# First feed-forward layer in blocks of 512 tokens, two blocks through half of the weights at a time

## The chip, the cores and the metric

The kernel runs on one core of a Trainium2 chip. The core's engines work side by side and meet at semaphores: TensorE (PE in the profile; PEld is its weight load), VectorE (DVE), ScalarE (ACT), GpSimd (POOL), and SyncE (SP), which here issues nearly all DMA transfers; 16 DMA engines carry them out. TensorE's results go to PSUM, eight banks of 512 float32 per partition. The metric is the device time of one execution in microseconds (us), of the slowest core; here there is only one.

## The reference

Attention with a forget gate, then two feed-forward layers, each over 2304 tokens of 512 features with 2048 hidden ones:

```python
def _attn_ref(q, k, v, f):            # 4 sequences, 8 heads, 576 tokens, 64 features per head
    scores = np.matmul(q, k.transpose(0, 1, 3, 2)) / np.sqrt(D)
    cum = np.cumsum(np.log(np.clip(f, 0.0001, 1.0)), axis=-1)
    decay = cum[:, :, :, None] - cum[:, :, None, :]
    scores = np.where(causal, -1000000000.0, scores + decay)
    ...
    return np.matmul(attn, v)         # attn: softmax of scores

def _moe_ref(x, w_in, w_out):         # layer one
    h = x @ w_in
    return (h * np.clip(h + 3.0, 0.0, 6.0) / 6.0) @ w_out

def _moe2_ref(x, w_in, w_out):        # layer two; beta = 1
    h = x @ w_in
    g = np.where(h >= 1, h, np.where(h <= -1, 0.0, (h + 1) ** 2 / 4.0))
    return g @ w_out
```

The weights come as 64-bit floats; the result is float32.

## The kernel before, in words

**Attention.** A sequence's 576 queries are cut into a first half of 256 (half 0) and the rest of 320 (half 1). `ORDER` lists the eight (sequence, half) groups in the order in which they are done. A group has four head pairs. An early pair (half 0) is one job: scores of both heads (`sc`), softmax on VectorE and ScalarE (lines 589 and 595), normalisation (`prob`, 667), transposes (`pt`, 682), and the product with v (`av`, 724). A late pair (half 1) is three jobs, with more scores and transposes and an `av` of ten matmuls. From `av` the pair's part of the next layer's input is written twice, rounded (`xt`, ACT line 371) and as the rest (DVE line 379). Score, transpose and `av` results take turns in two PSUM banks (`ps`); from step 34 on two more (`ps_b`) join them.

**Feed-forward.** Both layers are matrix products in fp32r, each factor split into a rounded part and its rest, so that three matmuls stand for one. The hidden features are 16 chunks of 128 (`NCH`). A step is one chunk of one block of tokens: `moe_h` makes `hp` (4 x 3 matmuls, line 811) and from it the gated `u` and its two parts `g`; `moe_o`, two steps later (`LAG`), adds the chunk's share to the block's output accumulators `o` (12 matmuls, line 852 in layer one, 859 in layer two). Layer one works in nine blocks of 256 tokens, layer two in four of 512 and one of 256. In layer one `hp` and `o` have a matmul width equal to the block (256); in layer two `hp` has 512 and `o` has the 512 output features. Finished accumulators go by `osb` to DRAM (`x2d`) and come back as layer two's input.

**Blocks 0 and 1** run interleaved, block 1 nine chunks behind (`STAG`); each of the others goes through all 16 chunks.

**Weights.** A chunk's input and output weights together fill one slot of `wsb`; there are 12, and 4 more when attention's buffers are free (`g7`, seven blocks done). The first time, a chunk comes raw as two halves of 64-bit numbers (`wraw`, 512 KB each) and is narrowed by one ScalarE and four VectorE operations (lines 428 to 439, tile `wr`), then rounded and split into the slot (`w`, one operation of each engine). `w_keep` stores the split chunk (`wf<-w`, 1 MB) if it is needed again; later loads are `w<-wf`. Layer two's halves are narrowed during layer one and kept in DRAM by GpSimd (`wf<-wr`).

**Order.** The program is written step by step, with attention's pieces dealt out between the half steps by their costs; `plan` then orders each engine's instructions by a list schedule with modelled costs (`graph`, `schedule`). The code below is that of the functions which the change touches; line numbers are the profile's.

Of the kernel before, what the change touches and what calls it, by code (L numbers as in the profile page):

```python
# [28 lines left out]
ORDER = ((0, 0), (1, 0), (2, 0), (0, 1), (1, 1), (3, 0), (2, 1), (3, 1))  # L29
# [8 lines left out]
SLOTS = 12  # L38
MORE = 16 - SLOTS
LAG = 2  # L40
STAG = 9
XT = 11
PRE0, PRE1 = 38, 106
WRAW = 4
AHEAD = 8100


def plan_weights(visits, avail):

# [185 lines left out]
def schedule(g, bw=330.0, fixed=3000.0, small=150.0):  # L235
# [20 lines left out]
    def when(k):  # L256
        t, need = ready[k], {}
        for name in g["users"][k]:
# [63 lines left out]
def tile_kernel(  # L322
# [71 lines left out]

    again = {}  # L400
# [688 lines left out]
```

## Time and profile before

| | us |
|---|---|
| median of 3 runs (1077.58 to 1081.18) | 1078.97 |
| the profiled execution, its own time | 1082.1 |
| its span, first to last instruction | 1080.1 |
| PE busy | 1028.2 (95%) |
| DVE busy | 597.6 (55%) |
| ACT busy | 544.6 (50%) |

The page's rows of 40 slices show the stages. A digit is a slice's busy share in tenths, PEclk the granted clock of TensorE:

```profile
PE   6796899989999999899999999999999999999998
DVE  6898995576677787678753447422422422332222
PEclk7697899999999999999999999999999999999999
DMA  6966595396596696865826035200200200010010
```

Each slice is 27 us. VectorE is fullest in the first six; TensorE from the fifth on. From about 580 us only feed-forward work is left, and layer two begins near 670 us. In the tables of stretches a row gives the stretch, its length, the busy us of PE, PEld, DVE, ACT and POOL with the number of instructions in brackets, then the granted clock, the share of the DMA engines and GB/s; where a line is named, only its engine's busy time is given. A matmul's own duration in a group overlaps its neighbours; what one costs in a dense stretch is read from the chain, where twelve in a row have one start and one length.

### The profile page before, as it was taken

What the parts mean: (1) busy time and instruction counts of PE and PEld (TensorE: products, weight loads), DVE (VectorE), ACT (ScalarE), POOL (GpSimd) and SP (SyncE); (2) the same over time, 40 slices, a digit from 0 to 9 for tenths busy, and PEclk for the clock granted to TensorE, in tenths of its full rate; (3) what the DMA queues carried; (4) which work ended last, traced back from release to release, by engine and by line L of the source; (5) the groups of instructions that cost most, each with busy time, mean ns of one, the idle gap of its engine ahead of it and who ended that gap; (6) DMA issues with size and microseconds to landing.
All of it is one profiled execution on the core that took longest, in us unless ns stands there. A gap on an engine that the chain in (4) does not pass through costs nothing.

```text
span 1080.1 us, 18043 instructions
## 1 busy us (share of the span) xinstructions
PE 1028.2 (95%) x6538; PEld 902.1 (84%) x6538; DVE 597.6 (55%) x1508; ACT 544.6 (50%) x1330; POOL 90.1 (8%) x223
## 2 busy tenths in 40 slices
PE   6796899989999999899999999999999999999998
PEld 4486799989888998798899999888888888888887
DVE  6898995576677787678753447422422422332222
ACT  5786775556556665556653235433333333333343
POOL 1100111011112111111111000000100100000000
PEclk7697899999999999999999999999999999999999
DMA  6966595396596696865826035200200200010010
GB/s 198 322 191 187 179 302 164 87 306 188 152 301 179 194 320 200 268 205 152 271 86 254 2 104 189 59 1 5 74 1 1 69 10 0 20 40 1 1 39 20
DMA packets 69784, 144.19 MB, mean 133 GB/s; under 512 B 11584, under 2 KB 38720, under 8 KB 65600
## 3 DMA queue, kind: packets, MB, share of 16 engines
q1 hardware_dynamic: 67136, 134.66, 40.5%
q0 software_dynamic: 2560, 8.39, 2.0%
q8 instruction: 51, 0.84, 0.3%
q14 instruction: 37, 0.30, 0.1%
HBM read 116.74 MB, written 26.29 MB: 132 GB/s over the span
## 4 chain that ended last, share of the span: by engine, by line
PE 74%; DMA 10%; DVE 8%; issue 2%; ACT 2%; SPq 0%; DVEq 0%; ACTq 0%
PE hp L811 32%; PE o L852 14%; PE o L859 10%; PE ps L859 8%; DMA kraw<-in_k 4%; PE av L724 3%; PE pt L682 3%; DMA dec<-ncum 3%; PE sc L638 2%; DMA x2d<-osb 1%; DVE prob L589 1%; DVE wr L436 1%; PE sc L613 1%; DMA wraw<-in_w 1%; DVE wr L439 1%
## 5 line engine op out<-in xcount | busy, mean ns | idle before, releaser
L811 PE MATMUL hp<-xt,w 128*128 128x256 f32 x1728 | 253.6, 291 | 3.4 <-DVE u L818 2.6
L852 PE MATMUL o<-g,w 128*128 128x256 f32 x1728 | 247.9, 289 | 1.4 <-ACT g L371 1.4
L811 PEld LDWEIGHTS hp<-xt,w 128*128 128x128 f32 x1728 | 227.7, 193 | 9.1 <-DVE u L818 1.8
L852 PEld LDWEIGHTS o<-g,w 128*128 128x128 f32 x1728 | 225.7, 192 | 4.9 <-ACT g L371 1.6
L811 PE MATMUL hp<-x,w 128*128 128x512 f32 (+1 forms) x960 | 211.2, 369 | 0.7 <-DVE u L822 0.7
L811 PEld LDWEIGHTS hp<-x,w 128*128 128x128 f32 x960 | 169.2, 188 | 33.5 <-DVE u L822 0.9
L822 DVE SCALAR_TENSOR_TENSOR u<-hp,u 128x512 f32<-128x512 f32 (+1 forms) x80 | 50.9, 638 | 210.2 <-ACT u L821 210.2
L379 DVE TENSOR_TENSOR g<-u,g 128x256 fp32r<-128x256 f32 (+1 forms) x224 | 112.3, 502 | 72.7 <-ACT g L371 72.1
L371 ACT ACTIVATE g<-u 128x256 fp32r<-128x256 f32 (+1 forms) x224 | 106.6, 476 | 87.5 <-DVE u L822 50.6
L820 ACT ACTIVATE u<-hp 128x512 f32<-128x512 f32 (+1 forms) x80 | 44.3, 554 | 196.5 <-PE hp L811 196.5
L859 PE MATMUL o<-w,g 128*128 128x512 f32 x480 | 124.8, 396 | 0.0
L859 PEld LDWEIGHTS o<-w,g 128*128 128x128 f32 x480 | 89.1, 188 | 19.8
L817 ACT ACTIVATE u<-hp 128x256 f32<-128x256 f32 x144 | 54.8, 380 | 99.7 <-PE hp L811 99.2
L595 ACT ACTIVATE prob<-prob,mx 128x384 f32<-128x384 f32 (+4 forms) x144 | 83.5, 581 | 34.6 <-DVE mx L589 33.6
L859 PE MATMUL ps<-w,g 128*128 128x512 f32 x384 | 100.3, 396 | 0.0
L818 DVE SCALAR_TENSOR_TENSOR u<-u,hp 128x256 f32<-128x256 f32 x144 | 60.0, 417 | 67.9 <-ACT u L817 67.3
L682 PE MATMUL pt<-ident,prob 128*128 128x128 f32 (+1 forms) x400 | 69.2, 293 | 21.5 <-DVE prob L667 6.9
L859 PEld LDWEIGHTS ps<-w,g 128*128 128x128 f32 x384 | 72.3, 189 | 17.5 <-ACT osb L869 0.3
L371 ACT ACTIVATE pt<-pt 128x512 f32<-128x512 f32 (+3 forms) x160 | 63.9, 432 | 25.5 <-PE pt L682 24.9
L589 DVE CUSTOM_DVE_ANT_0 prob<-sc,dec 128x256 f32<-128x256 f32 (+1 forms) x112 | 59.0, 535 | 24.7 <-PE sc L638 8.9
L682 PEld LDWEIGHTS pt<-ident,prob 128*128 128x128 f32 (+1 forms) x400 | 49.1, 149 | 27.3 <-ACT u L817 10.7
L724 PE MATMUL av<-pt,vv 128*64 128x320 f32 (+3 forms) x448 | 56.4, 381 | 1.1 <-DVE mx L589 1.1
(72 smaller groups left out, 958.9 us busy)
## 6 DMA issues: line engine op xcount, KB each, us to landing
wraw<-in_w SPq DMA_DIRECT2D x64, 512.0 KB
w<-wf SPq DMA_DIRECT2D x24, 1024.0 KB
dec<-ncum SPq DMA_DIRECT2D x45, 256.0 KB
kraw<-in_k SPq DMA_DIRECT2D x64, 144.0 KB
wf<-w SPq DMA_DIRECT2D x8, 1024.0 KB
wf<-wr POOLq DMA_DIRECT2D x32, 256.0 KB, 6.4
w<-wf SPq DMA_DIRECT2D x16, 512.0 KB
vv<-in_v SPq DMA_DIRECT2D x16, 320.0 KB
```

The lines of the kernel that those rows point to most:

```text
L371: nc.scalar.activation(out=out, in_=in_, func=AF.Copy)
L379: e.tensor_tensor(out=out, in0=in_, in1=hi.bitcast(F32), op=ALU.subtract)
L589: nc.vector.tensor_tensor_reduce(out=py[:, a:e], in0=s, in1=dc, scale=-0.125, scalar=mx[:, 2 * z:2 * z + 1] if x else 3.0e38, op0=ALU.add, ...
L595: nc.scalar.activation(out=py, in_=py, func=AF.Exp, scale=-1.0, bias=mx[:, 2 * z + x:2 * z + x + 1], accum_out=sm[:, z:z + 1],)
L682: nc.tensor.transpose(t[:nk, o:o + P], p[:, c:c + nk], ident)
L724: nc.tensor.matmul(t[y * D:(y + 1) * D, o:nq], lhsT=vv[:nk, y, c], rhs=rhs, start=c == 0, stop=c == nkc - 1,)
L811: nc.tensor.matmul(hp, lhsT=ws[:, a, k], rhs=x[:, bb, 0:w], start=(k == 0 and a == 0 and bb == 0), stop=(k == KD - 1 and bb == 1),)
L817: nc.scalar.activation(out=u, in_=hp, func=AF.Relu, bias=3.0, scale=1.0)
L818: nc.vector.scalar_tensor_tensor(out=u, in0=u, scalar=6.0, in1=hp, op0=ALU.min, op1=ALU.mult)
L822: nc.vector.scalar_tensor_tensor(out=u, in0=hp, scalar=1.0, in1=u, op0=ALU.max, op1=ALU.min)
L852: nc.tensor.matmul(o, lhsT=ws[:, a, KD + k], rhs=gg[:, bb], start=(n == 0 and k % 2 == 0 and a == 0 and bb == 0), stop=(n == NCH - 1 and b ...
L859: nc.tensor.matmul(acc[j][k], lhsT=gg[:, bb, k * P:(k + 1) * P], rhs=ws[:, a, KD:2 * KD].rearrange("p k n -> p (k n)"), start=(n == 0 and ...
```

## The change

Layer one gets the blocks 512, 512, 512, 256, 512. The first two go through half of the weights at a time: block 0 through chunks 0 to 7, block 1 through 0 to 7 and 8 to 15, block 0 through 8 to 15. So block 0's output is made in two parts, stored in two DRAM tensors and added when layer two reads them. All four groups of half 0 are attended first. Input and output weights have slots of their own, nine each (half the size), seven more each after attention; `w_keep` follows a chunk's second use. Layer one's outputs leave through `xt` buffers, and its four accumulators (`ps_o`) serve attention until the first step; after that attention has the two banks of `ps`. In `graph`, loads of raw weights and stores to `wf` count as ready only after the matmul written before them.

Line 811 becomes 822, 852 becomes 865, 371 becomes 378, 379 becomes 386, 436 and 439 become 439 and 442.

```diff
-T = 256
-NB = NT // T
+T1 = (512, 512, 512, 256, 512)
 T2 = (512, 512, 512, 512, 256)
+NB = len(T1)
 NB2 = NB + len(T2)
+WIDTH = T1 + T2
+FROM = [sum(T1[:j]) for j in range(NB)] + [sum(T2[:j]) for j in range(len(T2))]
...
-ORDER = ((0, 0), (1, 0), (2, 0), (0, 1), (1, 1), (3, 0), (2, 1), (3, 1))
+ORDER = ((0, 0), (1, 0), (2, 0), (3, 0), (0, 1), (1, 1), (2, 1), (3, 1))
...
-SLOTS = 12
-MORE = 16 - SLOTS
+SLOTS = (9, 9)
+OPEN = ((0, 0, 8), (1, 0, 8), (1, 8, 16), (0, 8, 16))
+LOOK = 5
 LAG = 2
-STAG = 9
+GO = 0
 XT = 11
-PRE0, PRE1 = 38, 106
-WRAW = 4
-AHEAD = 8100
-
-
...
+PRE = (17, 62)
+WRAW = 3
+AHEAD = 60000
+LEAD = (1, 1, 1, 1, 1, 1)
...
+    last = None
+    for k in range(n):
+        if eng[k] == "PE":
+            last = k
+        elif last is not None and type(ops[k]).__name__ == "InstDMACopy":
+            if any(x[0].startswith(held) for x in info[k][1]) if held else False:
+                deps[k].add(last)
...
-    ps_o = pool("ps_o", 1, PSUM)
     ps_h = pool("ps_h", 2, PSUM)
     ps_a = pool("ps", 2, PSUM)
-    ps_x = pool("ps_x", 1, PSUM)
-    ps_b = []
+    ps_o = pool("ps_i", 4, PSUM)
     turn = [0]
...
     def bank(name):
-        if name == "hp":
-            return ps_h.tile([P, 512], F32, tag="ps", name=name)
         turn[0] += 1
-        p = ps_b[0] if ps_b and turn[0] % 2 else ps_a
+        p = ps_h if name == "hp" else ps_o if turn[0] > 0 and turn[0] % 3 else ps_a
         return p.tile([P, 512], F32, tag="ps", name=name)
...
-    x2d = dram.tile([DM, NT], F32, name="x2d")
-    wf = [dram.tile([P, 2, 8, P] if c < NCH else [P, 8, P], F32, name=f"wf{c}") for c in range(2 * NCH)]
+    x2d = [dram.tile([DM, NT if x == 0 else T1[0]], F32, name=f"x2d{x}") for x in range(2)]
+    wf = [
+        [dram.tile([P, 2, 4, P] if c < NCH else [P, 4, P], F32, name=f"wf{c}_{x}") for x in range(2)]
+        for c in range(2 * NCH)
+    ]
...
-    wsb = [wpool.tile([P, 2, 8, P], F32R, name=f"w{s}") for s in range(SLOTS)]
+    wsb = [[wpool.tile([P, 2, 4, P], F32R, name=f"w{x}_{s}") for s in range(SLOTS[x])] for x in range(2)]
...
-    steps = []
-    for i in range(NCH + STAG):
-        if i < NCH:
-            steps.append((0, i, i))
-        if i >= STAG:
-            steps.append((1, i - STAG, i - STAG))
+    steps = [(j, c) for j, a, e in OPEN for c in range(a, e)]
     for j in range(2, NB2):
         order = range(NCH) if j % 2 else range(NCH - 1, -1, -1)
-        for n, c in enumerate(order):
-            steps.append((j, n, (j >= NB) * NCH + c))
-    g7 = (NB - 2) * NCH
-    where, loads = plan_weights([c for _, _, c in steps], [0] * SLOTS + [g7] * MORE)
-
-
-
-
+        steps += [(j, (j >= NB) * NCH + c) for c in order]
+    opens = [g for g in range(len(steps)) if g == 0 or steps[g - 1][0] != steps[g][0]]
+    closes = [g - 1 for g in opens[1:]] + [len(steps) - 1]
+    parts = {g: [steps[x][0] for x in opens[:n]].count(steps[g][0]) for n, g in enumerate(opens)}
+    g7 = (NB - 1) * NCH
...
+            full = lo.bitcast(F32)
+            if j == NB:
+                full, more = (moe.tile([P, 512], F32, tag="wr", name=f"part{y}", bufs=2) for y in range(2))
+            nc.sync.dma_start(out=full, in_=x2d[0][k * P:(k + 1) * P, t0:t0 + w])
+            if j == NB:
+                nc.sync.dma_start(out=more, in_=x2d[1][k * P:(k + 1) * P, t0:t0 + w])
+                nc.vector.tensor_tensor(out=full, in0=full, in1=more, op=ALU.add)
+            rounded("p", hi, full)
+            rest("v", lo, full, hi)
...
+        ws = wsb[0][where[0][g]]
+        hp = bank("hp")[:, 0:w]
...
+        j, c = steps[g]
+        n, last = g in opens, g in closes
+        if n:
+            part_of[j] = parts[g]
+        layer, t0, w = int(j >= NB), FROM[j], WIDTH[j]
+        ws = wsb[1][where[1][g]]
...
-        if n == 0:
-            acc[j] = [(ps_x if j == 1 else ps_o).tile([P, 512], F32, tag=f"o{k}", name=f"o{k}") for k in range(2)]
-            if layer:
-                acc[j] += [ps_b[0].tile([P, 512], F32, tag="ps", name="ps") for _ in range(T2[j - NB] // P - 2)]
+        m = 512 // w if layer == 0 else 1
+        if n:
+            nb = KD // m if layer == 0 else w // P
+            acc[j] = [ps_o.tile([P, 512], F32, tag=f"o{k}", name=f"o{k}") for k in range(nb)]
...
             for k in range(KD):
-                o = acc[j][k // 2][:, k % 2 * T:k % 2 * T + T]
+                o = acc[j][k // m][:, k % m * w:k % m * w + w]
                 for a, bb in ((0, 0), (1, 0), (0, 1)):
                     nc.tensor.matmul(
-                        o, lhsT=ws[:, a, KD + k], rhs=gg[:, bb], start=(n == 0 and k % 2 == 0 and a == 0 and bb == 0),
-                        stop=(n == NCH - 1 and bb == 1 and k % 2 == 1),
+                        o, lhsT=ws[:, a, k], rhs=gg[:, bb], start=(n and k % m == 0 and a == 0 and bb == 0),
+                        stop=(last and bb == 1 and k % m == m - 1),
                     )
...
-        if n == NCH - 1:
+        if last:
             for k in range(len(acc[j])):
-                o = moe.tile([P, 512], F32, tag="wr", name="osb", bufs=2)
+                if layer:
+                    o = moe.tile([P, 512], F32, tag="wr", name="osb", bufs=2)
+                else:
+                    if k % 2 == 0:
+                        pair = moe.tile([P, 2, 512], F32R, tag="xt", name="osb", bufs=XT)
+                    o = pair[:, k % 2].bitcast(F32)
...
                     nc.sync.dma_start(
-                        out=x2d[2 * k * P:2 * (k + 1) * P, t0:t0 + T].rearrange("(k p) n -> p k n", p=P),
-                        in_=o.rearrange("p (k n) -> p k n", k=2),
+                        out=x2d[part_of[j]][m * k * P:m * (k + 1) * P, t0:t0 + w].rearrange("(k p) n -> p k n", p=P),
+                        in_=o.rearrange("p (k n) -> p k n", k=m),
...
+    ps_o.close()
+    ps_o, turn[0] = pool("ps_o", 1, PSUM, reuse_waits="tile"), -(10 ** 9)
...
+            ext = pool("ext", 1, reuse_waits="tile")
+            for x in range(2):
+                wsb[x] += [ext.tile([P, 2, 4, P], F32R, name=f"w{x}_{s}", bufs=1) for s in range(SLOTS[x], 16)]
...
+            for side in range(2):
+                t = g - LAG * side
+                if t >= 0:
+                    (moe_o if side else moe_h)(t)
+                    c = steps[t][1]
+                    kept[c, side] = kept.get((c, side), 0) + 1
+                    if kept[c, side] == 2 and again[c, side]:
+                        w_keep(c, side, where[side][t])
+                while pos < len(seq) and cost[pos] < goal[2 * g + side] - 1:
...
-            if g == g7 + 20:
+            if g == g7 + 4:
                 moe_x(NB)
...
+    plan(tc, nc, homes, {"ext": "att", "ps_o": "ps_i"}, ("wraw", "wf"))
```

**TensorE's order where feed-forward work begins.** `hp` of step 0 is in `w_118` before and `w_0_145` now; `kn`, `qn` are keys and queries of early pairs. Before, the first `hp` follows the first `av` of the program:

```order
L628 MATMUL sc<-kn,qn 128x128 x2
L628 MATMUL sc<-kn,qn 128x256 x2
L724 MATMUL av<-pt,vv 64x256 x2
L724 MATMUL av<-pt,vv 64x128 x2
L682 MATMUL pt<-ident,prob_257 128x128
L682 MATMUL pt<-ident,prob_285 128x128
L682 MATMUL pt<-ident,prob_257 128x128
L682 MATMUL pt<-ident,prob_285 128x128
L811 MATMUL hp<-xt,w_118 128x256 x2
L682 MATMUL pt<-ident,prob_285 128x128 x2
L811 MATMUL hp<-xt,w_118 128x256
L811 MATMUL hp<-xt,w_119 128x256
```

Now:

```order
L632 MATMUL sc<-kn,qn 128x256
L686 MATMUL pt<-ident,prob_594 128x128 x2
L822 MATMUL hp<-xt,w_0_145 128x512
L632 MATMUL sc<-kn,qn 128x128
L822 MATMUL hp<-xt,w_0_145 128x512
L822 MATMUL hp<-xt,w_1_146 128x512 x2
L632 MATMUL sc<-kn,qn 128x128
L822 MATMUL hp<-xt,w_0_145 128x512
L728 MATMUL av<-pt,vv 64x256 x2
L728 MATMUL av<-pt,vv 64x128 x2
L822 MATMUL hp<-xt,w_1_146 128x512
L686 MATMUL pt<-ident,prob_686 128x128
```

The first `hp` is now 512 wide, and stands behind the `av` of the fifth pair (the two rows of `av` below it are the sixth) instead of the first.

**VectorE's order at the sixteenth half of the weights.** Before, that is the second half of chunk 7 (`w_125`, the lower of the two rows), with `u` and `g` 256 wide:

```order
L379 TENSOR_TENSOR w_125<-wr,w_125 128x512
L436 SCALAR_TENSOR_TENSOR wr<-wraw,wr 128x512
L379 TENSOR_TENSOR g<-u,g 128x256
L439 SCALAR_TENSOR_TENSOR wr<-wraw,wr 128x512
L429 TENSOR_SCALAR wr<-wr 128x512
L589 ISA prob_1061,mx<-sc,dm 128x128
L589 ISA mx 128x1
L433 TENSOR_SCALAR wr<-wr 128x512
L379 TENSOR_TENSOR kk<-kraw,kk 64x512
L379 TENSOR_TENSOR w_125<-wr,w_125 128x512
```

Now it is the output half of chunk 7 (`w_7_161`):

```order
L830 SCALAR_TENSOR_TENSOR u<-u,hp 128x512
L439 SCALAR_TENSOR_TENSOR wr<-wraw,wr 128x512
L830 SCALAR_TENSOR_TENSOR u<-u,hp 128x512
L442 SCALAR_TENSOR_TENSOR wr<-wraw,wr 128x512
L386 TENSOR_TENSOR g<-u,g 128x512
L593 ISA prob_1400,mx<-sc,dec 128x256
L593 ISA mx 128x1
L593 ISA prob_1400,mx<-sc,dec 128x256
L593 ISA mx 128x1
L386 TENSOR_TENSOR w_7_161<-wr,w_7_161 128x512
```

Ahead of this half stood six `g` of 256 and six `xt` before; now there are five `g` of 512 and twelve `xt`. The narrowing of the next half ends only behind the tenth `g`.

**SP's order among the loads of the first pairs.** `wraw` is a raw half, `wf<-w` a store of a split chunk. Before:

```order
L538 DMA dec<-ncum 128x2x256
L450 DMA wf_85<-w_118 128x2048
L499 DMA kn<-in_k 128x256
L501 DMA qn<-in_q 64x256
L476 DMA vv<-in_v 128x2x128
L538 DMA dec<-ncum 128x2x256
L407 DMA wraw<-in_w 128x1024
L501 DMA qn<-in_q 64x256
L407 DMA wraw<-in_w 128x1024
L450 DMA wf_86<-w_119 128x2048
```

Now, at the same pairs' `dec` loads:

```order
L480 DMA vv<-in_v 128x2x128
L411 DMA wraw<-in_w 128x1024
L542 DMA dec<-ncum 128x2x256
L411 DMA wraw<-in_w 128x1024
L480 DMA vv<-in_v 128x2x128
L542 DMA dec<-ncum 128x2x256
L480 DMA vv<-in_v 128x2x128
L411 DMA wraw<-in_w 128x1024 x2
L480 DMA vv<-in_v 128x2x128
L542 DMA dec<-ncum 128x2x256
```

No store stands among these loads any more; the first one comes at row 94 of SP, behind the first loads of late pairs.

## Rows read from the trace of the kernel before

**Rows 1.** Stretches of the program: us, busy us by engine, granted clock, DMA.

```profile
0.00:135.00 135.00, 106.91 (x599) 86.69 (x600) 113.49 (x324) 93.43 (x253) 16.96 (x39) 0.80 0.69 215
30.00:150.00 120.00, 100.28 (x654) 85.71 (x653) 110.04 (x299) 88.72 (x240) 15.36 (x25) 0.83 0.71 225
120.00:200.00 80.00, 79.69 (x646) 75.43 (x645) 60.91 (x173) 51.56 (x143) 10.29 (x22) 1.00 0.61 191
135.00:580.00 445.00, 425.89 (x3325) 390.79 (x3324) 316.05 (x913) 266.56 (x745) 59.88 (x164) 0.99 0.69 211
580.00:670.00 90.00, 90.00 (x752) 90.00 (x751) 44.12 (x83) 35.34 (x76) 5.17 (x8) 1.00 0.36 121
```

**Rows 2.** The same view of line 811 (`hp` of layer one) alone.

```profile
0.00:135.00 135.00, 35.65 (x185) 29.75 (x186) 0.80 0.69 215
135.00:580.00 445.00, 166.54 (x1161) 149.87 (x1160) 0.99 0.69 211
```

**Rows 3.** The same of line 852 (`o` of layer one).

```profile
0.00:135.00 135.00, 25.77 (x156) 22.83 (x156) 0.80 0.69 215
135.00:580.00 445.00, 167.32 (x1164) 151.54 (x1164) 0.99 0.69 211
```

**Rows 4.** The same of line 724 (`av`).

```profile
135.00:580.00 445.00, 45.02 (x368) 23.09 (x368) 0.99 0.69 211
```

**Rows 5.** Chain of work, start us, us, what; layer one.

```profile
180.07 2.35 PE av L724 x20
184.05 1.44 PE o L852 x12
185.49 1.44 PE hp L811 x12
```

**Rows 6.** The chain in layer two.

```profile
692.75 2.73 PE hp L811 x12
695.48 1.40 PE o L859 x6
```

**Rows 7.** Groups by line and form, whole program: busy us, mean ns.

```profile
L811 PE MATMUL hp<-xt,w 128*128 128x256 f32 x1728 | 253.6, 291 | 3.4 <-DVE u L818 2.6 <-ACT w L371 0.4 <-DVE w L379 0.3
```

**Rows 8.** Groups by form, VectorE, 0 to 135 us.

```profile
L429 DVE TENSOR_SCALAR wr<-wr 128x512 f32<-128x512 f32 x27 | 11.5, 428 | 0.8 <-ACT wr L428 0.6
L433 DVE TENSOR_SCALAR wr<-wr 128x512 int32<-128x512 int32 x26 | 11.4, 440 | 0.2
L439 DVE SCALAR_TENSOR_TENSOR wr<-wraw,wr 128x512 int32<-128x512 int32 x26 | 17.9, 690 | 0.1
L379 DVE TENSOR_TENSOR w<-wr,w 128x512 fp32r<-128x512 f32 x26 | 18.2, 699 | 3.6 <-ACT w L371 3.2 <-ACT prob L665 0.2
L589 DVE CUSTOM_DVE_ANT_0 prob<-sc,dec 128x256 f32<-128x256 f32 x22 | 8.9, 420 | 3.0 <-issue 1.8 <-PE sc L628 1.0
L589 DVE CUSTOM_DVE_ANT_0 prob<-sc,dm 128x128 f32<-128x128 f32 x24 | 6.5, 281 | 1.4 <-PE sc L628 0.8 <-PE sc L638 0.6
L589 DVE DVE_READ_ACCUMULATOR2_ANT mx<- 128x1 f32 x46 | 3.8, 82 | 0.0
L667 DVE TENSOR_SCALAR prob<-prob,rd 128x128 f32<-128x128 f32 x22 | 5.7, 292 | 0.0
L379 DVE TENSOR_TENSOR kk<-kraw,kk 64x512 fp32r<-64x512 f32 x4 | 2.8, 690 | 0.1
L379 DVE TENSOR_TENSOR xt<-av,xt 128x256 fp32r<-128x256 f32 x10 | 4.1, 410 | 0.9 <-ACT xt L371 0.9
L379 DVE TENSOR_TENSOR g<-u,g 128x256 fp32r<-128x256 f32 x15 | 6.3, 423 | 0.0
```

**Rows 9.** Groups by form, VectorE, whole program, 512 wide.

```profile
L379 DVE TENSOR_TENSOR g<-u,g 128x512 fp32r<-128x512 f32 x64 | 44.3, 693 | 43.1 <-ACT g L371 43.0
```

**Rows 10.** Waits of TensorE, 120 to 580 us: total, times, longest us.

```profile
PE pt L682 <- ACT sum L657: 5.1, 1, 5.1
```

More of the change, by code (lines that the diff above doesn't have):

```diff
@@ L55, in plan_weights @@
         last[visits[t]] = t
-    n = len(avail)
     held, where, loads = {}, [], []
-    chunk, nuse, used = [None] * n, [10**9] * n, [a - LAG - 1 if a else -LAG - 1 for a in avail]
+    chunk, nuse = [None] * n, [10**9] * n
+    used = [-lag - 1] * slots + [more[1] - lag - 1] * more[0]
     for t, c in enumerate(visits):
         if c not in held:
-            ok = [x for x in range(n) if used[x] + LAG + 1 <= t]
+            ok = [x for x in range(n) if used[x] + lag + 1 <= t + lag]
             empty = [x for x in ok if chunk[x] is None]
@@ L261, in when @@
             tag = g["where"][name]
-            if turn[name] > got.get(tag, 0):
+            if turn[name] > got.get(tag, 0) or g["first"][name] != k:
                 return None
@@ L417, in w_split @@
         if kind == "whole":
[L418 to L420 removed]
+            hi, lo = wsb[half][s][:, 0], wsb[half][s][:, 1]
+            rounded("a", hi, lo.bitcast(F32))
+            rest("v", lo, lo.bitcast(F32), hi)
             return
[L422 removed]
         r = moe.tile([P, 4, P], F32, tag="wr", name="wr", bufs=2)
@@ L923, in tile_kernel @@
     wq, seen = [], set()
-    for c, s, free, need in loads:
+    for c, x, s, free, need in sorted(loads, key=lambda r: r[4]):
         assert free <= need
         if c >= NCH:
-            wq.append((free, min(free + 4, need - 2), "whole", c, None, s))
-        elif c in seen:
-            wq.append((free, free, "parts", c, None, s))
-        else:
-            seen.add(c)
-            t = free if free > 0 else max(-1, need - 6)
-            wq += [(t - 3, t, "raw", c, half, s) for half in range(2)]
-    first = list(dict.fromkeys(c for c, _, _, _ in loads if c >= NCH))
+            wq.append((free, min(free + 4, need - 2), "whole", c, x, s))
+        elif (c, x) in seen:
+            wq.append((free, free, "parts", c, x, s))
+        else:
+            seen.add((c, x))
+            t = max(free if free > 0 else -1, need - LOOK)
+            wq.append((t - 3, t, "raw", c, x, s))
+    first = list(dict.fromkeys(c for c, _, _, _, _ in loads if c >= NCH))
+    span = [WIDTH[j] for j, _ in steps]
+    part = [sum(span[:g]) for g in range(len(steps) + 1)]
     for n, c in enumerate(first):
-        t = PRE0 + (PRE1 - PRE0) * n // NCH
+        x = part[PRE[0]] + (part[PRE[1]] - part[PRE[0]]) * n // NCH
+        t = [g for g in range(len(steps)) if part[g] <= x][-1]
         wq += [(t - 3, t, "raw", c, half, None) for half in range(2)]
@@ L994, in tile_kernel @@
     weights_until(-1)
-    spans = [(0, STAG, 1), (STAG, 2 * NCH, 2)] + [(j * NCH, (j + 1) * NCH, j + 1) for j in range(2, NB)]
+    spans = [(0, 8, 1), (8, 32, 2)] + [(j * NCH, (j + 1) * NCH, j + 1) for j in range(2, NB)]
     cost = [sum(x[0] for x in seq[:n]) for n in range(len(seq) + 1)]
@@ L1004, in tile_kernel @@
         left = cost[-1] - cost[n0]
-        share = cost[n0] + left * (e - a) / (g7 - a) if e <= g7 else cost[-1]
+        share = cost[n0] + left * LEAD[x] * (part[e] - part[a]) / (part[g7] - part[a]) if e < g7 else cost[-1]
         aim = max(cost[due[x]], min(share, cost[due[x]] + AHEAD))
-        aim = max(aim, cost[n0]) if x else cost[due[x]]
+        aim = max(aim, cost[n0])
         for y in range(n2):
@@ L1017, in tile_kernel @@
             att.close()
[L1018 to L1019 removed]
+            ext = pool("ext", 1, reuse_waits="tile")
+            for x in range(2):
+                wsb[x] += [ext.tile([P, 2, 4, P], F32R, name=f"w{x}_{s}", bufs=1) for s in range(SLOTS[x], 16)]
         weights_until(g)
         if g < n1:
[L1022 to L1030 removed]
+            for side in range(2):
[7 more added lines that the diff above has]
+                while pos < len(seq) and cost[pos] < goal[2 * g + side] - 1:
                     seq[pos][1]()
                     pos += 1
[L1033 to L1036 removed]
+            if g == g7 + 4:
                 moe_x(NB)
[L1038 to L1040 removed]
         else:
             if g < len(steps):
[L1043 removed]
                 moe_h(g)
[L1045 to L1046 removed]
+                if g - 4 in opens and steps[g][0] + 1 < NB2:
+                    moe_x(steps[g][0] + 1)
             moe_o(g - LAG)
[L1048 to L1049 removed]
+    plan(tc, nc, homes, {"ext": "att", "ps_o": "ps_i"}, ("wraw", "wf"))
+    for x in (ext, ps_o, ps_a, ps_h, dram, moe, wpool, const):
         x.close()
```

111 lines of the change are left out of this document (41 added, 70 removed).

## The prediction

> **What bounds the kernel now.** I read busy time and granted clock in stretches first, then single matmul groups in the chain, then VectorE by form, then TensorE's waits. The stretches [rows 1] show two regimes. From 135 us on TensorE is the bound: 425.9 of 445 us busy up to 580, where attention ends, and all of 580 to 670. Before that it is VectorE: 110.0 of 120 us busy between 30 and 150, while TensorE's granted clock is 0.83 in the mean, so part of that time is at the lower of its two levels (1.2 instead of 2.4 GHz). Little of the bound engine's work gets done there: by 135 us 185 + 156 matmuls of layer one [rows 2, 3], 41 us at 120 ns each, and 10 head pairs (the 10 `xt` of [rows 8]). So there are two questions: what the change takes from TensorE's dense part, and what from VectorE's start.
>
> **The change, part by part. Wider matmuls.** Twelve matmuls of 256 columns take 1.44 us, 120.0 ns each, for `hp` and for layer one's `o` alike [rows 5]; twelve of 512 take 2.73 us, 227.5 ns [rows 6]. Two narrow ones cost 12.5 ns more than one wide. Layer one has 1728 narrow ones for `hp` [rows 7] and as many for `o`; four blocks of 512 turn 3072 of the 3456 into 1536 wide ones, the block of 256 keeps 384. Saved: 1536 x 12.5 ns = 19.2 us, 4.8 of them (384 wide ones) in the last block, behind attention, 14.4 before. No row shows layer one's `o` at 512. Its operands lie as those of `hp`, so I take 227.5; layer two's `o` needs 1.40 us for six, 233.3 ns [rows 6], and at that end 768 x 5.8 ns = 4.5 us of the 19.2 are lost again. That it is no gain at all is excluded as long as the shape behaves like one of these two.
>
> The Trainium skill, TensorE: Matmul & The Clock Gate, section Back-to-back issue gap, gives N/2.4 + 2.5 ns between matmuls at the full clock. By that the fixed part is 2.5 ns instead of 12.5, and the same sum would be 1536 x 2.5 = 3.8 us. The rows disagree with it at a granted clock of 1.00, so it is only a rival below.
>
> **VectorE's start.** Before, block 0 needs all 16 weight chunks, 32 halves, in its 16 steps of 256 tokens; now 8 chunks last until 1024 tokens have gone through them. A half costs VectorE 0.428 + 0.440 + 2 x 0.690 + 0.699 = 2.95 us [rows 8]. By 135 us it had done 26 halves and 15 steps. In the new order 16 halves stand ahead of the eighth `g` (eight steps of 512, a little more than fifteen of 256), with 14 `xt`, 33 + 32 softmax pieces and 9 `kk` and `ql` (before: 10, 22 + 24, 5), so much of the fifteenth and sixteenth pair too. By the means of [rows 8, 9]: 10 halves, -29.5; softmax 11 x 0.420 + 8 x 0.281 + 19 reads x 0.082 = +8.4; 4 x 2 x 0.690 = +5.5; 4 `xt` x 0.410 = +1.6; 14 more scalings of 0.292 or somewhat longer, +4.4; `u` and `g` 8 x 2 x 0.693 - 15 x 2 x 0.423 = -1.6. Net -11.2; I take 10, because neighbours on VectorE overlap a little. Step 8 then ends near 125 us with four more pairs through attention. Never waiting, VectorE would be there at its own 113.5 us busy [rows 1] less 10, 103; with nothing gained, 135.
>
> The first `hp` [the two orders of TensorE above] now needs `xt` of two groups of attention, so until the fifth pair there is no feed-forward work to fill TensorE. I cost that at nothing while VectorE is the later one: five pairs with five halves are some 30 us of it. If TensorE were the later one it would cost what is done of `hp` before that, 30-odd matmuls, 4 us. That the stores of split weights (`wf<-w`) leave the queue of SP in this stretch can only help; under VectorE's cover I price it at nothing.
>
> **From step 8 to the end of attention.** Before, from 135 to 580 us, TensorE's 425.9 us [rows 1] were 1161 + 1164 narrow matmuls [rows 2, 3], 279.0 us, and 146.9 us of attention. Its 368 `av` records [rows 4] are 6 early pairs of 8 and 16 late ones of 20 (early: queries 0 to 255 of a sequence; late: the rest). An early `av` has 768 columns of the 2432 that take 2.35 us in a late one [rows 5], 0.7 us; with scores and transposes of 2048 columns at about the same rate or less, 2.2 us a pair. A late pair is then (146.9 - 13.2)/16 = 8.4 us. After: of the 48 x 24 = 1152 wide matmuls before the last block 96 + 72 are done at step 8; 984 x 227.5 ns = 223.9 us; 384 narrow ones, 46.1; less the 24 that were still due at 580 before, 2.9; two early pairs 4.4; sixteen late ones 133.8: 405.3 us. With idle time in proportion as before (445/425.9) 423.5 us, and attention ends at 125 + 423.5 = 548.5 instead of 580: 31.5 us less.
>
> What may spoil that is VectorE: the order puts 16 full and 14 shorter halves (no rounding, 2.25 us) between the eighth and the 32nd `g`, 78.7 us against 203 us of TensorE, 0.39 of it. From 135 to 580 before, the 38 halves left of 64 were 89.7 us, 0.20, of a busy share of 0.71. So VectorE comes to 0.90 in these 203 us: under the bound, but close.
>
> **Layer two and the seam** keep their shapes. The two parts of block 0 are added on VectorE (4 x 0.69 us) in layer one's last block, where VectorE is busy 44 of 90 us [rows 1]; without that cover they would cost 2.8 us.
>
> **Sum:** 31.5 + 4.8 = 36.3 us off the profiled execution's 1082.1 (span 1080.1 and 2.0 around it): 1045.8. The median of the runs lies 3.1 us under that execution, so 1043.
>
> **Rivals.** (a) *The start is given back.* VectorE saturates in steps 8 to 32 and TensorE sinks to its share of 30 to 150 us, 100.3/120 = 0.84 [rows 1]: 194 us of work take 232 instead of 203, so 1043 + 29 = 1072. For it: the 0.90 above; against: in the start the pipeline was also empty and the clock low. (b) *Slower: two banks for attention.* Ahead of the feed-forward part attention has six PSUM banks, but from block 0 on only the two of `ps`, where before it has four from step 34 on. A late pair uses 13 banks (6 scores, 6 transposes, 1 `av`). If each of 16 x 13 = 208 uses makes TensorE wait w, the gain is gone at w = 0.17 us; at 0.3 us it is 1043 + 62 = 1105. Against it: from 120 to 200 us attention had two banks as well, and TensorE was busy 79.7 of 80 us [rows 1]. For it: TensorE's waits for softmax ahead of `pt`, one of 5.1 us [rows 10]. (The Trainium skill, Perfetto Trace Analysis, section Matmuls, wants independent groups to rotate through different banks so that evacuation overlaps; the change shortens that rotation. In the stretch with two banks the trace shows no harm from it.) (c) *The idle time of the middle goes too*: 405.3 us without it, 18 less, 1025. For it: loads of half the size hold the queue for less time; against: the wait in [rows 10] hangs on softmax. (d) *A fixed cost of 2.5 ns per matmul*: 15.4 us less saved, 1058.
>
> **Chances:** the forecast 0.46 (own range 1030 to 1059), (a) 0.26, (b) 0.09, (c) 0.16, (d) 0.03. A difference under 0.3% (3.2 us) can't be told from none. Slower 0.09, from (b); same 0.04, from the tails of (a) and (b); faster 0.87. The range holds the forecast, (c), (d) and most of (a), with layer one's `o` at its dearer end: 1013 to 1073.
>
> **What would show it.** Twelve wide matmuls in 2.73 us in layer one, `o` too; VectorE at its eighth `g` near 125 us with 16 halves done; some 200 us from there to step 32; the last `xt` near 547 us; no rise of TensorE's waits ahead of `sc`, `pt` and `av`. It is wrong if the first `hp` comes much after 60 us, if VectorE is full after step 8 and TensorE is not, or if TensorE waits for an evacuation in every step.

## The result, and the profile after

The changed kernel takes 1038.85 us (median of 4 runs, 1035.11 to 1043.95), the kernel before beside it 1078.74: a ratio of 0.963, 95% interval 0.9575 to 0.9686. The profiled execution took 1042.43 us with a span of 1040.7, 39.4 less than before. The forecast was 1043, and 1045.8 on the profiled execution's own scale.

The first line of the page after: busy time, share of the span and instructions of each engine.

```profile
PE 1002.5 (96%) x5002; PEld 802.5 (77%) x5002; DVE 586.5 (56%) x1390; ACT 527.0 (51%) x1208; POOL 94.6 (9%) x223
```

Next the view by stretches, with the columns of [rows 1]. The last three are cut at events: from the eighth to the 32nd `g` of VectorE, from there to the last `xt`, from there to the first `hp` of layer two.

```profile
0.00:135.00 135.00, 121.44 (x584) 84.14 (x585) 110.13 (x349) 102.21 (x299) 20.65 (x50) 0.85 0.59 170
125.00:341.20 216.20, 202.23 (x1022) 155.50 (x1019) 173.99 (x434) 132.18 (x321) 30.77 (x78) 0.98 0.75 238
341.20:554.80 213.60, 206.85 (x1233) 168.07 (x1232) 143.86 (x372) 117.19 (x294) 31.07 (x79) 0.99 0.73 230
554.80:637.80 83.00, 83.00 (x379) 69.20 (x378) 44.42 (x68) 35.77 (x62) 2.66 (x3) 1.00 0.55 186
```

Two rows of the chain stand for each layer, first layer one, then layer two; they answer to [rows 5] and [rows 6].

```profile
366.38 2.72 PE hp L822 x12
369.10 2.72 PE o L865 x12
...
692.22 2.72 PE hp L822 x12
694.94 2.72 PE o L872 x12
```

Where did the 39.4 us go? Three cuts, each read from the two traces: the last `xt` ends at 554.8 us instead of 578.6 (-23.8); from there to layer two's first `hp` it is 82.9 instead of 93.6 (-10.7); layer two takes 403.1 instead of 408.0 (-4.9). The first two come to 34.5 where the forecast had 36.3. The third was not forecast at all: the six `o` of layer two that took 1.40 us in [rows 6] now take 1.36, twelve of them 2.72.

Two views answer to the forecast's signs. VectorE up to its eighth `g`, by form, as in [rows 8]:

```profile
L439 DVE SCALAR_TENSOR_TENSOR wr<-wraw,wr 128x512 int32<-128x512 int32 x16 | 11.2, 702 | 0.1
L386 DVE TENSOR_TENSOR xt<-av,xt 128x256 fp32r<-128x256 f32 x14 | 5.8, 414 | 1.4 <-ACT xt L378 1.4
L386 DVE TENSOR_TENSOR g<-u,g 128x512 fp32r<-128x512 f32 x8 | 5.7, 709 | 0.5 <-ACT g L378 0.5
```

and TensorE's waits from 120 to 560 us, as in [rows 10]:

```profile
PE pt L686 <- DVE prob L671: 10.9, 4, 4.0
PE sc L642 <- ACT pt L378: 3.9, 3, 2.7
PE pt L686 <- DVE mx L593: 3.0, 1, 3.0
PE sc L617 <- DVE mx L593: 2.2, 2, 1.2
```

In the kernel before, the same stretch has 18.7 us of waits ahead of `pt` and `sc`; the longest group is

```profile
PE pt L682 <- DVE prob L667: 6.9, 5, 2.2
```

Sixteen halves and fourteen `xt` stand ahead of the eighth `g`, as the order had it, and that `g` starts at 124.7 us. The waits after come to 20 us, hardly more than before, and none is longer than 4.0.

### The profile page after: what moved, and what is told of

Its sections match the earlier page's. It is cut to its first block, busy times and chain, and to the rows that moved or that the text cites. A ratio compares the mean times of both kernels' runs of the same rounds, so it can differ in the third digit from the quotient of the medians.

```text
span 1040.7 us, 14773 instructions
## 1 busy us (share of the span) xinstructions
PE 1002.5 (96%) x5002; PEld 802.5 (77%) x5002; DVE 586.5 (56%) x1390; ACT 527.0 (51%) x1208; POOL 94.6 (9%) x223
## 4 chain that ended last, share of the span: by engine, by line
PE 80%; DMA 11%; DVE 4%; ACT 3%; issue 1%; SPq 0%; POOL 0%; DVEq 0%; POOLq 0%; ACTq 0%
PE hp L822 34%; PE o L872 19%; PE o L865 14%; DMA dec<-ncum 6%; DMA wraw<-in_w 4%; PE av L728 4%; PE pt L686 4%; PE sc L642 3%; PE sc L632 1%; DVE prob L593 1%; PE sc L617 1%; ACT prob L599 1%; DMA wf<-wr 1%; DVE wr L439 1%; ACT wr L431 0%
## 5 line engine op out<-in xcount | busy, mean ns | idle before, releaser
L822 PE MATMUL hp<-xt,w 128*128 128x512 f32 (+1 forms) x960 | 237.5, 383 | 1.7 <-DVE xt L386 0.6
L865 PE MATMUL o<-g,w 128*128 128x512 f32 (+1 forms) x960 | 233.7, 379 | 0.0
L872 PE MATMUL o<-w,g 128*128 128x512 f32 x864 | 209.2, 390 | 0.0
L822 PEld LDWEIGHTS hp<-xt,w 128*128 128x128 f32 x960 | 168.7, 193 | 31.8 <-issue 1.5
L865 PEld LDWEIGHTS o<-g,w 128*128 128x128 f32 x960 | 166.9, 190 | 28.3 <-issue 0.7
L872 PEld LDWEIGHTS o<-w,g 128*128 128x128 f32 x864 | 160.9, 188 | 33.2 <-ACT osb L887 0.7
L386 DVE TENSOR_TENSOR g<-u,g 128x512 fp32r<-128x512 f32 (+1 forms) x160 | 102.3, 640 | 69.2 <-PE o L872 35.0
L378 ACT ACTIVATE g<-u 128x512 fp32r<-128x512 f32 (+1 forms) x160 | 94.0, 589 | 77.2 <-DVE u L834 50.9
L599 ACT ACTIVATE prob<-prob,mx 128x128 f32<-128x128 f32 (+4 forms) x144 | 83.3, 579 | 54.5 <-DVE mx L593 54.1
L686 PE MATMUL pt<-ident,prob 128*128 128x128 f32 (+1 forms) x400 | 72.9, 297 | 17.1 <-DVE prob L671 13.3
L830 DVE SCALAR_TENSOR_TENSOR u<-u,hp 128x512 f32<-128x512 f32 (+1 forms) x80 | 50.4, 630 | 59.6 <-ACT u L829 59.2
L686 PEld LDWEIGHTS pt<-ident,prob 128*128 128x128 f32 (+1 forms) x400 | 50.9, 149 | 36.3 <-DVE prob L671 15.4
L593 DVE CUSTOM_DVE_ANT_0 prob<-sc,dec 128x256 f32<-128x256 f32 (+1 forms) x112 | 58.6, 534 | 34.5 <-DMA dec<-ncum 15.2
```

Of the source, the lines that this page charges most:

```text
L378: nc.scalar.activation(out=out, in_=in_, func=AF.Copy)
L386: e.tensor_tensor(out=out, in0=in_, in1=hi.bitcast(F32), op=ALU.subtract)
L593: nc.vector.tensor_tensor_reduce(out=py[:, a:e], in0=s, in1=dc, scale=-0.125, scalar=mx[:, 2 * z:2 * z + 1] if x else 3.0e38, op0=ALU.add, ...
L599: nc.scalar.activation(out=py, in_=py, func=AF.Exp, scale=-1.0, bias=mx[:, 2 * z + x:2 * z + x + 1], accum_out=sm[:, z:z + 1],)
L686: nc.tensor.transpose(t[:nk, o:o + P], p[:, c:c + nk], ident)
L822: nc.tensor.matmul(hp, lhsT=ws[:, a, k], rhs=x[:, bb, 0:w], start=(k == 0 and a == 0 and bb == 0), stop=(k == KD - 1 and bb == 1),)
```

## The experiments

Times are medians. "The changed kernel" is 1038.85 as first timed; beside e11 it was 1037.55.

**e1: how wide a matmul is.** Each 512-wide matmul of layer one becomes two of 256 (`hp` is shown; `o` likewise).

```diff
-  nc.tensor.matmul(hp, lhsT=ws[:, a, k], rhs=x[:, bb, 0:w], ...)
+  for z in range(2):
+      nc.tensor.matmul(hp[:, 256*z:256*z+256], lhsT=ws[:, a, k], rhs=x[:, bb, 256*z:256*z+256], ...)
```

> The changed kernel (median 1038.85 us), but each of the 1536 matmuls of 512 tokens in layer one (and the 256-token ones stay) is issued as two of 256 into the two halves of the same bank: 3072 starts more by 1536. Theory of the forecast: a matmul carries a fixed 12.5 to 13.3 ns beside its columns (120.0 ns at 256, 226.7 at 512 in the trace), so wherever TensorE sets the pace each pair costs 240 in place of 227: 1536 x 12.5 to 13.3 ns = 19 to 20.5 us, less what falls into the first 32 of the 64 wide steps where VectorE holds TensorE: if the half of it that stands in these steps is hidden, 10 us. Whole time 1049 to 1059 us; from the 33rd g to the last xt 12 matmuls of a step in 2.88 in place of 2.72 us. Rival: the fixed part is only some 2.5 ns (the Trainium skill, Tensor Engine, on the gap between back-to-back matmuls): +4 us, 1043. Rival: the gain came from somewhere else and width is worth nothing: 1039.

Measured: 1057.77 us, 18.9 more than the changed kernel. The chain behind attention shows the price; in a row of 24, two narrow matmuls stand for a wide one:

```profile
567.51 2.88 PE hp L824 x24
574.71 2.88 PE o L874 x24
```

2.88 against 2.72 us is 13.3 ns for each pair, and 1536 pairs are 20.5. Width alone is half of the whole gain. A fixed 2.5 ns is out for these matmuls, and with it the rival built on it. (The Trainium skill, TensorE: Matmul & The Clock Gate, section Back-to-back issue gap, gives the 2.5 ns for an isolated matmul, and says that in a stream of weight loads and matmuls both set the spacing. The trace shows 13.3 ns where each matmul brings new weights.) Every matmul here has a weight load of its own, so the runs don't tell what part of the 13.3 ns is the load's. Nothing of it was hidden in the stage from the eighth to the 32nd `g` either: it grew from 216.4 to 225.6 us, and 24 steps of 24 pairs at 13.3 ns are 7.7.

**e2: all of the weights at once.** The order of the steps is shown; with it go the addition of the two parts of block 0, the use after which a chunk is stored, and the stretches over which attention is dealt out.

```diff
-    steps = [(j, c) for j, a, e in OPEN for c in range(a, e)]
+    steps = [(0, c) for c in range(NCH)] + [(1, c) for c in range(NCH - 1, -1, -1)]
...
```

> The changed kernel, but block 0 goes through all 16 chunks at once and then block 1 through the 16 in reverse (the addition of two parts of block 0 at the start of layer two falls away, under 1 us of layer two). Theory: the first 16 steps then need all of the weights from the start, twice as much to narrow and split on VectorE before the 16th step, while the attention that block 1 needs comes later; by the sums of VectorE's rows, g 8, 16, 24, 32, 48 at 112, 190, 239, 304, 387 us against 111, 169, 239, 289, 381 in the changed kernel by the same sums. So the 16th g is 20 us later, the 24th at the same time, the 32nd 15 later, the 48th 6 later, and TensorE's wait goes from steps 16 to 24 to steps 8 to 16: whole time 0 to 10 us longer, 1039 to 1049. Rival: going through half of the weights is what gave the start its gain, and what is lost there is never made up: 15 to 25 us longer, 1054 to 1064. Rival: the order makes no difference at all, since the same work is on VectorE by the 32nd step: 1039 within 2 us and the 32nd g at the same time as in the changed kernel (334 us).

Measured: 1078.93 us, the whole gain lost, more than any theory gave. The `g` 8, 16, 24, 32, 48 start at 123.1, 212.2, 280.8, 398.6 and 517.1 us; in the changed kernel at 124.7, 201.4, 272.6, 341.2 and 475.7. My sums over VectorE had the 16th 20 us later and the 24th at the same time; they are 11 and 8 us later. What they missed lies between the 24th and the 32nd, which took 49 us more. Some 19 of these are work that only stands there (an estimate: 20 `av` more, one late pair at the forecast's 8.4 us, and 46 matmuls of layer one at 227 ns); the rest of the delay stays, and layer two's first `hp` comes 35 us later. The stretches show TensorE idle and at a lower granted clock:

```profile
150.00:180.00 30.00, 18.78 (x85) 12.66 (x83) 26.23 (x68) 18.33 (x43) 2.90 (x8) 0.72 0.62 187
300.00:330.00 30.00, 20.53 (x82) 14.56 (x82) 17.71 (x49) 12.35 (x33) 5.93 (x13) 0.77 0.61 180
360.00:390.00 30.00, 21.07 (x78) 15.40 (x77) 12.95 (x28) 10.02 (x23) 3.73 (x11) 0.77 0.58 180
```

In the first of them VectorE is busy 26.2 of 30 us, as the theory had it. In the last it is not, and the chain there ends in weights read back:

```profile
356.44 10.96 DMA w<-wf
386.38 6.48 DMA w<-wf
```

Sixteen chunks at a time through nine slots need 54 of these 512 KB loads in place of 40. Up to 630 us TensorE is idle 54.7 us instead of 34.3, and the mean granted clock of the span is 0.958 instead of 0.974, so 18 us more are lost to the clock (1075.7 x 0.042 less 1040.7 x 0.026). But 8 of these 18 fall into time in which TensorE was idle anyway; over its busy time the clock took 35.5 us instead of 25.9. So 20 us of idle time and 10 of clock stand against 35 of span. A theory of one engine was not enough: half of the weights at a time also saves loads. How much of the 35 us hangs on the loads is not shown: from 280 to 400 us TensorE's own waits for `w<-wf` are 6.1 us of some 24 idle, and the new deal of attention was not tested by itself.

**e3 and e4: two banks for attention.** From step 34 on the kernel before gives attention four banks, two of `ps` and two of `ps_b` (the "three" of the second expectation is a slip). e3 takes over the planner's two rules (`g["first"][name] != k`, and a read of PSUM by another engine as a dependence), e4 also this:

```diff
-        p = ps_b[0] if ps_b and turn[0] % 2 else ps_a
+        p = ps_a
```

> The kernel before with the two rules of the planner that came with the change (a tile may be taken only by the first instruction that uses it; a read of a PSUM tile by another engine counts as a dependence) and nothing else: the control for the next one. Theory: the rules decide nothing at most places: 1079 us within 0.5%. Rival: the rules themselves change the order enough to gain or lose over 1%.

> As e3, but attention has only two PSUM banks in place of three from the start of layer one on, as in the changed kernel. Theory: in the changed kernel's trace TensorE waits no longer for banks than before (pt<-prob 10.9, sc<-pt 3.9, pt<-mx 3.0, sc<-mx 2.2 us between 120 and 560), so two banks cost nothing here either: the time of e3 within 0.5%. Rival of the forecast: each use of a bank waits some tenth of a microsecond more, up to 40 us: slower by over 1%, with waits of pt and sc on VectorE and ScalarE to match.

Measured: 1076.82 us, ratio to the kernel before 0.999 (0.9978 to 1.0002), and 1075.02, ratio 0.9969 (0.9954 to 0.9983). In the kernel before, two banks cost nothing; for the changed kernel this is carried over. The waits ahead of `pt` and `sc` from 120 to 560 us, first of e4,

```profile
PE pt L682 <- DVE mx L589: 4.1, 3, 2.3
PE sc L638 <- ACT pt L371: 3.6, 2, 3.2
PE pt L682 <- DVE prob L667: 3.4, 1, 3.4
```

are no more than what e3 shows ahead of `pt` alone:

```profile
PE pt L682 <- DVE prob L667: 11.1, 8, 2.2
```

**e5 and e6: why layer two's `o` got faster.** The compiled programs put `g` of layer two at bytes 217056, 221152 and 225248 of a partition before, at 139904, 144000 and 148096 after. Both experiments pad each `g` buffer by 32 bytes, which moves some of the three:

```diff
-  gg = moe.tile([P, 2, 512], F32R, tag="g", name="g", bufs=3)[:, :, 0:w]
+  gg = moe.tile([P, 2 * 512 + 8], F32R, tag="g", name="g", bufs=3)
+  gg = gg[:, 0:1024].rearrange("p (a n) -> p a n", a=2)[:, :, 0:w]
```

> The kernel before, with 32 bytes of padding behind each of the three g buffers of layer two. Their starts were all 32 past a multiple of 64 bytes (217056, 221152, 225248 within a partition); now two of the three start at a multiple of 64 and the middle one stays at 32 past it. Theory A (the -4.9 us of layer two that the forecast had at nothing come from where g, the weights' side of o, starts): in the o of layer two the 12 matmuls of a chunk take 2.72 us for two chunks of three and 2.80 for the third; 2/3 x 864 x 7 ns = 4 us shorter, 1074 us. Theory B (they come from the weights' slots, whose rows in before are halves of 8 KB slots, or from the banks): all chunks stay at 2.80 and the time at 1078.5.

> The changed kernel with the same padding behind its g buffers: the middle one of three, and the weight slots 9 to 15 of both sides (which exist in layer two alone and lie behind), then start 32 past a multiple of 64. Theory A: o of layer two at 2.80 us for one chunk in three and 2.72 for the others; hp of layer two at 2.80 for the chunks whose w lies in slots 9 to 15, 7 of 16, and 2.72 for the rest: 864/3 x 7 + 768 x 7/16 x 7 ns = 2.0 + 2.4, 4.4 us longer, 1043. Theory B: nothing changes, 1039.

Measured: e5 1075.27 us (ratio 0.9954, 0.9936 to 0.9972), e6 1047.46. So the address of `g` matters, and theory B is out. But the rule that I had written down is wrong: in e5 one chunk in three is fast, not two. That its time came out as forecast is luck: layer two is only 2.6 us shorter in its trace (405.4), the median 4.0, and the rest is not explained. e6, 8.6 us longer instead of 4.4, misses its forecast: layer two takes 409.5 instead of 403.1, and layer one has slow matmuls of 512 too, since its `g` and its last block's weights lie in the same places. Its chain (the twelve `o` of a chunk stand as six and six, since two banks belong to another pool):

```profile
696.45 1.40 PE o L863 x6
697.84 1.40 PE ps L863 x6
...
701.97 1.36 PE o L863 x6
703.33 1.36 PE ps L863 x6
...
707.41 1.40 PE o L863 x6
```

The fast buffer is the one at 216960; 225216 is slow, though it is a multiple of 64. 216960 is one of 128, 225216 is not, and all three of the changed kernel are. With 128 in place of 64 e6 fits too: one `g` of three starts at a multiple of it, and the slots 9 to 15 of `w` do not, so `hp` is slow where its weights lie in them, and `o` where its moving side does:

```profile
696.73 2.81 PE hp L822 x12
699.54 2.79 PE o L873 x12
...
774.91 2.72 PE hp L822 x12
777.63 2.72 PE o L873 x12
```

A single matmul of 512 starts 227 ns after the one ahead of it if both of its operands start at a multiple of 128 bytes, and 229 to 235 (medians by case) if one does not.

**e10: the rule put to the test.** This padding stands once beside the kernel before's `g` buffers, so that they lie at 216960, 221056 and 225152:

```diff
+        if layer and not padded:
+            padded.append(ffn.tile([P, 24], F32, tag="pad", name="pad", bufs=1))
+            nc.gpsimd.memset(padded[0], 0.0)
```

> The kernel before, with 96 bytes of padding ahead of layer two's g buffers, once, so that all three start at a multiple of 128 bytes within a partition (225152, 221056, 216960; in before all are 96 past one). After e5 and e6, where 12 matmuls of 512 took 2.72 us if both of their operands started at a multiple of 128 and 2.76 to 2.82 otherwise (a multiple of 64 alone did not do): all chunks of o in layer two take 2.72 in place of 2.81, 864 x 6.7 ns = 5.8 us shorter, 1073. Rival (the rule is some other one that e5 and e6 happen to fit, the slots of w for instance): o stays at 2.76 or more for some or all chunks, and the time above 1076.

Measured: 1073.87 us, ratio 0.995 (0.9933 to 0.9968), 5.2 less than the kernel before. All chunks run at

```profile
692.26 1.36 PE o L862 x6
693.62 1.36 PE ps L862 x6
694.98 2.72 PE hp L811 x12
```

and layer two takes 401.6 us in place of 408.0. So the unforeseen 4.9 us came with the addresses that the changed kernel's pools happen to give to `g`.

**e7, e8, e9: what the stage after the start is short of.** e7 moves the halves of layer two's weights behind step 32; e8 leaves VectorE's part of them out; e9 leaves out seven eighths of the bytes that they load.

```diff
 # e7
-PRE = (17, 62)
+PRE = (32, 62)
 # e8, before the four operations of VectorE
+        if s is None:
+            nc.gpsimd.dma_start(out=wf[c][half], in_=r)
+            return
 # e9, for halves of layer two
+                nc.sync.dma_start(out=raw[:, 0:n], in_=w[c // NCH, c % NCH, :, 8 * P * half:8 * P * half + 2 * n])
+                return raw[:, 0:n].unsqueeze(1).to_broadcast([P, 8, n, 2])
...
```

> The changed kernel, but the 32 halves of layer two's weights are fetched and narrowed from step 32 to step 62 in place of 17 to 62. Theory (VectorE, over 0.9 busy in long stretches from the eighth to the 32nd g, held TensorE there: 216 us in place of the 203 that TensorE needs): the 14 halves, 31 us of VectorE, leave this stage; the 32nd g comes at about 328 in place of 341, the work fits between steps 32 and 62, where VectorE was 0.7 busy, and the whole is 6 to 13 us shorter, 1026 to 1033. Rival: what TensorE waits for in that stage is transfers that stand late in SyncE's queue (dec, kraw, w); then the 32nd g stays within 4 us of 341, and the time within 3 us of 1039. Rival on the other side: 32 halves in 30 steps are too many where kept chunks are read back too; the stage from 32 to 64 gets longer by more than is gained, 1042 to 1050.

> The changed kernel without the four VectorE operations that narrow a half of layer two's weights (2.25 us, 32 halves, 72 us of VectorE between steps 17 and 62); their loads, ScalarE's part and the stores stay, so layer two computes with wrong weights. Theory that VectorE held TensorE: the 32nd g at about 328 in place of 341 and the last xt 15 to 25 us earlier, 1015 to 1028 us. Rival that transfers and their queue did: the 32nd g and the last xt within 4 us of before this edit, 1035 to 1040.

> The changed kernel, but each of the 32 loads for layer two's narrowing brings an eighth of its bytes (64 KB in place of 512), and the narrowing reads these eight times over, so that VectorE, ScalarE and the stores do as much as before and layer two computes with wrong weights. It is the counterpart of e8, which took VectorE's part away and left the loads. Theory after e7 and e8 (of the 12.5 us that e7 took out of the stage from the eighth to the 32nd g, e8 gave 4; the rest are the loads, which fill the DMA queues in front of dec, kraw and w): the stage is 207 to 210 us in place of 216, and the whole 3 to 8 us shorter, 1031 to 1036. Rival (the loads cost nothing, the rest of e7's gain came from ScalarE's part, the stores on POOL or the order): stage 214 to 218, the whole within 2 us of the changed kernel.

Measured: 1033.88, 1033.95 and 1027.87 us. The stage from the eighth to the 32nd `g` took 204.0 us in e7, 212.5 in e8 and 215.0 in e9, against 216.4 (214.8 in e12, the changed kernel once more, so differences of 2 us are nothing). The two stretches of e8, up to the 32nd `g` and on to the last `xt`,

```profile
124.00:335.80 211.80, 200.88 (x1026) 155.99 (x1023) 151.85 (x386) 133.16 (x322) 29.86 (x81) 0.97 0.79 248
335.80:541.90 206.10, 202.28 (x1192) 165.29 (x1193) 106.01 (x289) 112.68 (x287) 25.66 (x76) 0.99 0.74 235
```

and of e9:

```profile
122.00:336.40 214.40, 202.58 (x1030) 155.91 (x1027) 176.33 (x442) 132.29 (x324) 31.63 (x81) 0.98 0.68 213
336.40:535.80 199.40, 197.06 (x1186) 162.50 (x1185) 139.86 (x361) 113.28 (x287) 27.06 (x76) 1.00 0.67 204
```

In e8 VectorE loses 22 us of work in this stage and the stage only 2 to 4; in e9 the DMA engines go from 0.75 to 0.68 and the stage stays. So the theory that VectorE alone held TensorE there is wrong, and so is mine for e9 that the loads did. Both edits pay later: from the 32nd `g` to the last `xt` it is 7.5 us less in e8 and 14.2 in e9 (e12 has 3.6 more there than the first trace, so the 14.2 are clear and the 7.5 less so). Only e7, which takes the halves away whole, takes 10 to 12 us out of the stage. In the chain of the changed kernel the DMA waits of this stage are

```profile
131.85 10.95 DMA wraw<-in_w
182.96 13.77 DMA wraw<-in_w
211.28 10.60 DMA wraw<-in_w
...
263.03 10.06 DMA dec<-ncum
273.75 6.16 DMA wf<-wr
288.47 12.77 DMA dec<-ncum
```

e7 keeps the first and has none of these others:

```profile
126.93 10.62 DMA wraw<-in_w
252.35 7.62 DMA qraw<-in_q
275.79 6.56 DMA x2d<-osb
...
```

What e8 and e9 leave in place is the turn that the halves of both layers take in the three `wraw` buffers and in SyncE's queue. That this is what layer one's loads wait for fits e9, where a wait of 13.05 us for `wraw` at 179 us is still in the chain. It does not fit e8 as well: there the chain keeps only the first of the `wraw` waits, and the stage is nearly as long. It was not tested by itself and stays open.

**e11 and e12: e7 and the changed kernel again, side by side.**

> e7 again, on one chip with the changed kernel (e12) and in five rounds, since the two medians (1033.9 and 1038.85) lie within each other's spread. If moving the layer-two halves behind step 32 is worth what its profile showed (last xt 16 us earlier, span 12 us shorter) or what its median showed (5 us): ratio to the kernel before 0.955 to 0.959, 4 to 8 us below e12. If it was chance: the same as e12.

> The changed kernel again, beside e11, in five rounds: 1037 to 1041 us, ratio 0.961 to 0.966.

Measured: 1031.52 us, ratio 0.9566 (0.9538 to 0.9595), and 1037.55, ratio 0.9627 (0.9599 to 0.9654). Moving layer two's halves behind step 32 is worth 6.0 us, with intervals that just do not meet: a version that beats both kernels. The two profiled executions differ by more (spans of 1029.8 and 1043.0), since e12's is the slowest of its six, so their stages overstate the gain. e11's stage and the stretch behind it:

```profile
121.30:325.40 204.10, 196.80 (x1027) 153.12 (x1023) 155.96 (x396) 129.22 (x311) 21.57 (x68) 0.99 0.67 207
325.40:541.60 216.20, 211.28 (x1239) 170.73 (x1236) 157.36 (x400) 119.27 (x297) 32.48 (x85) 0.99 0.80 256
```

TensorE is idle 7.3 us in the stage instead of 14.0, and the second stretch carries the 14 more halves at no more than 216.2 us, against 217.3 in e12. From there to layer two TensorE is idle 4.4 of 85.3 us, where the changed kernel had no idle time, so part of the gain is given back.

## Why the prediction was right, and where it was off

**Wider matmuls.** Forecast 12.5 ns a pair, 19.2 us. The chain has 2.72 us for twelve, so 13.3 ns and 20.5 us, and e1 gave 18.9 back. Layer one's `o` came out at `hp`'s price. The dearer end, layer two's `o` at 233.3 ns, was not a matter of the operation at all but of where `g` lay (e10). The change without its width is e1: 1057.8 against 1078.7, so the new order brought the other half, with layer two's 4.9 us in it.

**VectorE's start.** Forecast: the eighth `g` near 125 us, with 16 halves. Measured 124.7, with 16. VectorE's busy time up to there is 102.6 us, where the forecast had 113.5 less 10. The first `hp` at 44.7 us, 15 later than before, cost nothing that can be seen: in e1 it starts at 24.6, and the eighth `g` at 124.6 all the same.

**From step 8 to layer two.** The work was sized right, its place was not. I had 405.3 us of TensorE's work up to the last `xt` and, with the 4.8 saved, 87.4 behind it: 492.7. The three stretches hold 202.2 + 206.9 + 83.0 = 492.1. I had 18.2 us of idle time; it is 14.0 + 6.7 + 0 = 20.7. But the step "some 200 us from there to step 32" failed: 216.4. TensorE had 202 us of work there, not 194, and was idle 14 us, not 9. The granted clock of 0.98 is some 4 us of the 8 (216.2 x 0.02); the pairs are not more than the 194 held (156 `av`: two early, seven late), and where the rest comes from is open, as is what held the stage (e7 to e9). The last `xt`, forecast near 547, came at 554.8. The stretches behind the stage were shorter by nearly as much, which was luck: no term of the forecast set one off against the other. So layer two's first `hp` came at 637.7, where the forecast's terms give 635.9.

**Layer two.** "Keep their shapes" and so no change: a term put at nothing that was 4.9 us. The shape is the same, the addresses are not, and these set 227 or 234 ns. That they fell well was luck.

**The sum.** 1045.8 forecast for the profiled execution, +1.8 at layer two's first `hp`, -4.9 in layer two, -0.3 around the span (1.7 us instead of 2.0): 1042.4.

**The rivals.** (a), the start given back: the stage was 13 us longer than forecast, but not for (a)'s reason. VectorE was busy 174 of 216 us, 0.80 and not 0.90, TensorE 0.94 and not 0.84, and with 22 us less on VectorE (e8) the stage stayed nearly as long. (b), two banks: no sign of it (the waits after, and e4). (c), no idle time at all: no, though e7 shows that a part of it was to be had. (d): out by e1.

## What to carry to other kernels

A matmul with its weight load has a price beside its columns: count matmuls, and make them as wide as the bank allows, before looking for idle time; here that was half of the gain. Check the stage cut of a forecast apart from its sum: mine was within 2 us at layer two's start, with one stage on the way wrong by 13. After a change of the pools, compare where the operands start: the same instruction was 3% dearer at another address. And work for a later stage that stands among scarce loads is best moved whole to where the engines have room: taking away only its arithmetic or only its bytes left that stage nearly as it was (the stretch behind it did gain).

## What the runs showed of the hardware

The start of an operand within a partition matters to TensorE. At 512 columns of fp32r with new weights each time, matmuls follow each other in 227 ns if the weights and the moving side both start at a multiple of 128 bytes, and in 233 to 235 with the weights 96 past it (the kernel before; e10 brought that to 227). A multiple of 64 alone gave 235 in one `g` buffer of e5. At 256 columns the kernel before shows 120.0 ns with the moving side of layer one off such a multiple and its weights on one, the same as after with both on one, so for that width no price of the moving side is to be seen.

Stalls cost more than their idle time in e2: 20.4 us more of it came with a mean granted clock lower by 0.016; over TensorE's busy time that is 35.5 us lost to the clock instead of 25.9, 10 us more.
